# A soft mixture-of-experts behind linear attention: a fourth home for early weights, the last experts' products ahead of the first half's last chunks, 512-column zero products

## The chip, the core and the metric

The kernel runs on one core of a Trainium2 chip. The metric is the device time of one execution in microseconds, median of several runs. Before the change it is 177.03 us (three runs, 176.82 to 177.19).

## The reference

For 8 batches and 8 heads (sequence 576, head dimension 64) linear attention is computed, normalised, and handed as 4,608 tokens of 512 features to a soft mixture of 8 experts with 4 slots each. All data is 4-byte floating point.

```python
kv = np.einsum('bhsd,bhse->bhde', k, v)
out = np.einsum('bhsd,bhde->bhse', q, kv)
rms = np.sqrt(np.mean(out * out, axis=-1, keepdims=True) + 1e-06)
x = out / rms * g_norm                      # as 4608 tokens x 512
logits = x @ phi                            # 4608 x 32 slots
d = softmax(logits, over the tokens)
slot_input = d.T @ x                        # 8 experts x 4 slots x 512
h = np.maximum(slot_input[e] @ w1[e], 0.0)  # 512 x 1024 per expert
slot_out[e] = h @ w2[e]                     # 1024 x 512 per expert
c = softmax(logits, over the slots)
return c @ slot_out
```

## The kernel before, in words

The core reads 61.9 MB (k, v, q and the weights `w1`, `w2` of 4 MB per expert) and writes 9.4 MB. The work has two parts.

**The token part** goes over 36 tiles of 128 tokens (`products`, `square`, `evict` and what follows them). TensorE multiplies q by the block matrices `bds[0]` and `bds[1]`, ScalarE and VectorE find the norms, GpSimd scales, and the tokens of a group of six tiles are summed into slots (`group_sum`, L361) against a running maximum. The last group is the serial piece: its maximum is found (L317), transposed on TensorE (`pm`, L327), broadcast (`pb`, L342), subtracted and put through the exponential, and only then come the group's 48 small products (L361), their transpose (`psT`, L504) and the first expert. `fill` (L398) puts products of zeros on TensorE where it would otherwise stand idle: `EARLY` at the start, `LATE_FILL` in that serial piece. The first entry of `LATE_FILL` is 28 products of 256 columns, started when the sums of the group before are done; the next instruction of TensorE behind them is `pm`.

**The expert part** computes `expert_h(e)` (L567, from `w1`) and `expert_y(e, hf)` (L585, from `w2`, `hf` one half of the 512 output features). For the first four experts both halves of y follow at once; for the last four, half 0 comes first. Then `mix(0)` copies the sums out of PSUM (VectorE), spreads them with one product (`pz`, L602) and copies them back (`z`, L604). `output(hf, k, f)` makes one chunk of the result: two products pairs (`po`, L613), one copied by ScalarE (L621), one by VectorE (L623), into a tile `st`, and one transfer of 768 KB (L624). There are 12 chunks, six for each half. The table `late` places the last four `expert_y(e, 1)` between the first half's chunks; `mix(1)` follows all six.

**Transfers.** All of them are issued by SyncE in one order that is written out in the code: k, v and q, then the weights of experts 0 to 3, `w1` of 4 to 7, half 0 of `w2` of 4 to 7, half 1, and then the results as they come. SyncE works in order and waits for the semaphore of the transfer issued eight before, so at most eight are under way. Buffers: `ring` has 17 slots of 1 MB through which k, v, q, the weights and then the result tiles go; a new tile waits until the tile 17 before has been used. `w1` is loaded in two blocks of 1 MB per expert, k = 0 and 1. Three blocks don't use the ring: block (4, 0) lies in four 256 KB pieces in the small pool `rest` (`SPLIT`), and (5, 0) and (5, 1) in eight pieces in the token tiles `xts` that are done with (`IN_X`). `load_w1` (L72) issues all of them; a piece has rows of 2 KB, a whole block rows of 8 KB.

Of the kernel before, what the change touches and what calls it, by code (L numbers as in the profile page):

```python
# [8 lines left out]
F32 = mybir.dt.float32  # L9
# [5 lines left out]
P = 128  # L15
# [3 lines left out]
NE = 8  # L19
# [7 lines left out]
NCH = NT // CT  # L27
NX = 14
EARLY = (18, 2, 0)
LATE_FILL = (28, 5, 5, 2, 2)  # L30
PACED = 3
SLOT = 2048
NSLOT = 17
SPLIT = (4, 0)
IN_X = ((5, 0), (5, 1))
NREST = 5
EPS_RMS = 1e-6
EPS_SUM = 1e-9
# [3 lines left out]
def soft_moe_linear_attention(ctx: ExitStack, tc: tile.TileContext, kv_in, kvr_in, q_in, qr_in, w1_in, w2_in, c_in, out):  # L42


    nc = tc.nc

    const = ctx.enter_context(tc.tile_pool(name="const", bufs=1))
    ring = ctx.enter_context(tc.tile_pool(name="ring", bufs=NSLOT))
    rest = ctx.enter_context(tc.tile_pool(name="rest", bufs=NREST))
    wk = ctx.enter_context(tc.tile_pool(name="wk", bufs=2))  # L50
# [20 lines left out]

    def load_w1(e):  # L72
        for k in range(2):
            if (e, k) == SPLIT or (e, k) in IN_X:

                if (e, k) == SPLIT:
                    parts = [rest.tile([P, 512], F32, tag="rest", name=f"w1_{e}_{k}_{i}") for i in range(4)]
                else:
                    T = NT - GROUPS[-1] - 8 + 4 * IN_X.index((e, k))
                    parts = [xts[(T + i) % NX].rearrange("p j n -> p (j n)")[:, :512] for i in range(4)]  # L80
                for i, t in enumerate(parts):
                    nc.sync.dma_start(t, w1_in[e, k, :, i // 2, i % 2 * 512 : i % 2 * 512 + 512])
                w1_sb[e, k] = [[parts[2 * c + j // 2][:, j % 2 * 256 : j % 2 * 256 + 256] for j in range(4)] for c in range(2)]
                continue
            t = ring.tile([P, 2, FF], F32, tag="ring", name=f"w1_{e}_{k}")
            nc.sync.dma_start(t, w1_in[e, k])
            w1_sb[e, k] = [[t[:, c, j * 256 : (j + 1) * 256] for j in range(4)] for c in range(2)]
# [19 lines left out]
    zeros = const.tile([P, 256], BF16, name="zeros")  # L107
# [13 lines left out]
    bds = [const.tile([P, NPAIR, 192], F32, name=f"bd{i}") for i in range(2)]  # L121
# [3 lines left out]
    for i in range(NX):  # L125
        t = const.tile([P, 4, 129], F32, name=f"x{i}")
# [12 lines left out]
    ps = psA.enter_context(tc.tile_pool(name="psA", bufs=1, space=bass.MemoryType.PSUM))  # L139
# [69 lines left out]
    sqs, mss, parts, r0s, rs_of = {}, {}, {}, {}, {}  # L209
# [74 lines left out]
    def scale_o(T, o, of_x):  # L284

        s = stage_of[T]
        r = rs_of[s][:, T - starts[s]].rearrange("p (j w) -> p j w", w=2).unsqueeze(3)
        if of_x:
            out = xts[T % NX][:, :, :128].rearrange("p j (w d) -> p j w d", w=2)
            src = o[:, :, 32:160].rearrange("p j (w d) -> p j w d", w=2)  # L290
        else:
            parts[s] = wk.tile([P, STAGES[s], H, NS], F32, tag="part", name=f"part{s}", bufs=3)
            out = parts[s][:, T - starts[s]].rearrange("p (j w) n -> p j w n", w=2)
            src = o[:, :, :192].rearrange("p j (c n) -> p j c n", n=NS)[:, :, 0::5]
        nc.vector.tensor_tensor(out=out, in0=src, in1=r.to_broadcast([P, 4, 2, D if of_x else NS]), op=ALU.mult)
# [28 lines left out]
    def group_max_T(G):  # L324
        pm = ps.tile([P, P], F32, tag="m", name=f"pm{G}")
        for j in range(4):
            nc.tensor.matmul(  # L327
                pm[32 * j : 32 * j + 32], lhsT=L[:, pos(g0[G]) + GROUPS[G]], rhs=ident, start=True, stop=True
            )
        pms[G] = pm  # L330
# [9 lines left out]
    def group_exp_PE(G):  # L340
        pbs[G] = ps.tile([P, NS], F32, tag="m", name=f"pb{G}")
        nc.tensor.matmul(pbs[G], lhsT=ones, rhs=held[G], start=True, stop=True)  # L342
# [12 lines left out]
    def group_sum(G, i):  # L355
        if i == 0:
            sums[G] = ps.tile([P, 129], F32, tag="s", name=f"pS{G}")
        pS = sums[G]
        x = xts[(g0[G] + i) % NX]
        for j in range(4):  # L360
            nc.tensor.matmul(  # L361
                pS[32 * j : 32 * j + 32], lhsT=ds[G][:, i], rhs=x[:, j], start=i == 0, stop=i == GROUPS[G] - 1
            )
        if i == GROUPS[G] - 1:
            if G == 0:
                nc.vector.tensor_copy(out=acc, in_=pS)
            else:
                nc.vector.scalar_tensor_tensor(
                    out=acc, in0=acc, scalar=alphas.pop(G), in1=pS, op0=ALU.mult, op1=ALU.add
                )  # L370
# [27 lines left out]
    def fill(n, cols=256, home=None):  # L398

        if not n:  # L400
            return
        t = home if home is not None else ps.tile([P, 2, 512], F32, tag="o", name="fill", bufs=2)[:, 1]
        for i in range(n):
            nc.tensor.matmul(t[:, :cols], lhsT=zeros[:, :P], rhs=zeros[:, :cols], start=True, stop=True)

    fill(EARLY[0])

# [8 lines left out]
    for T in range(NT - 2):  # L416
# [15 lines left out]
        old = ends.get(T - 2)  # L432
# [50 lines left out]
    group_max(G)  # L483
    for i in todo_sums:
        group_sum(*i)
    fill(LATE_FILL[0], home=ps.tile([P, 256], F32, tag="m", name="fill"))
    group_max_T(G)
    group_max_row(G)
    group_diag(G)
    scale_o(A, oA, True)  # L490
    fill(LATE_FILL[1], home=tail_ps[:, 1])
    group_exp_PE(G)
    group_exp(G)
    scale_o(Z, oZ, True)
    fill(LATE_FILL[2], home=tail_ps[:, 1])
    for i in range(GROUPS[G]):
        group_sum(G, i)
    fill(LATE_FILL[3], home=tail_ps[:, 1])

# [4 lines left out]
    nc.tensor.transpose(psT, acc[:, :128], ident)  # L504
    fill(LATE_FILL[4], home=tail_ps[:, 1])
    mine = psT.rearrange("p (j e k) -> p e j k", j=4, k=SPE)
# [17 lines left out]
    ps = ctx.enter_context(tc.tile_pool(name="psB", bufs=3, space=bass.MemoryType.PSUM, reuse_waits="tile"))  # L524
    LATE = 4
# [55 lines left out]
    def expert_y(e, hf):  # L581
        w2 = w2_sb[e, hf]
        for c in range(8):
            j = c % 4
            nc.tensor.matmul(  # L585
                pY[32 * j : 32 * j + 32, hf, :256],
                lhsT=hTs[e][:, c],
                rhs=w2[:, c],
                start=e == 0 and c < 4,
                stop=e == NE - 1 and c >= 4,  # L590
            )
# [5 lines left out]
    def mix(hf):  # L597

        y = wk.tile([P, 256], F32, tag="part", name=f"y{hf}", bufs=3)
        nc.vector.tensor_copy(out=y, in_=pY[:, hf, :256])  # L600
        pz = ps.tile([P, 2, 512], F32, tag="m", name=f"pz{hf}")[:, 0, :256]
        nc.tensor.matmul(pz, lhsT=sel.rearrange("p a n -> p (a n)"), rhs=y, start=True, stop=True)  # L602
        zs[hf] = wk.tile([P, 256], F32, tag="part", name=f"z{hf}", bufs=3)
        nc.vector.tensor_copy(out=zs[hf], in_=pz)  # L604

    def output(hf, k, f):
        z = zs[hf]
        st = ring.tile([P, 4, CT * NS], F32, tag="ring", name=f"st{hf}_{k}_{f}")
        for v in range(2):
            po = ps.tile([P, 2, 512], F32, tag="m", name=f"po{hf}_{k}_{f}_{v}")  # L610
            for u in range(2):
                lo = 32 * (2 * v + u)
                nc.tensor.matmul(  # L613
                    po[:, u, : CT * NS].rearrange("p (g x) -> p g x", g=2),
                    lhsT=z[lo : lo + 32, f * P : (f + 1) * P],
                    rhs=cT[k][lo : lo + 32],
                    start=True,
                    stop=True,
                )
            if v == 0:  # L620
                nc.scalar.copy(st[:, 0:2], po[:, :, : CT * NS])  # L621
            else:
                nc.vector.tensor_copy(out=st[:, 2:4], in_=po[:, :, : CT * NS])  # L623
        nc.sync.dma_start(out[hf, k, f], st)  # L624
# [20 lines left out]
            keep_busy(PACED)  # L645
    mix(0)
    chunks = [(k, f) for k in range(NCH) for f in range(2)]
    late = {1: 0, 2: 1, 4: 2, 5: 3}
    for i, (k, f) in enumerate(chunks):
        output(0, k, f)  # L650
        if i in late:
            expert_y(NE - LATE + late[i], 1)
    mix(1)
    for k, f in chunks:
        output(1, k, f)

# [1 line left out]
def build_program():  # L658
    import concourse.bacc as bacc

    nc = bacc.Bacc("TRN2", target_bir_lowering=False, num_devices=1)
    shapes = {"kv": (B, 2, P, SLOT), "kr": (B, P, 512), "qt": (B, P, NPAIR, 512), "qr": (B // 2, P, 2, NPAIR, 64), "w1": (NE, 2, P, 2, FF), "w2": (NE, 2, P, 8, 256), "cs": (P, 129)}
    args = [nc.dram_tensor(f"in_{n}_dram", s, F32, kind="ExternalInput").ap() for n, s in shapes.items()]
    args.append(nc.dram_tensor("out_0_dram", (2, NCH, 2, P, 4, CT * NS), F32, kind="ExternalOutput").ap())
    with tile.TileContext(nc, schedule_with_timeline_sim=True) as tc, tc.manual_schedule():
        soft_moe_linear_attention(tc, *args)
    return nc
# [40 lines left out]
```

## Time and profile before

| | |
|---|---|
| median of the runs | 177.03 us (176.82 to 177.19) |
| profiled execution: time, span | 176.62 us, 174.8 us |
| busy, share of the span | PE 86%, VectorE 51%, ScalarE 50%, GpSimd 32% |
| transfers | 71.69 MB, mean 410 GB/s; SyncE's queue 98.6% of 16 engines |
| TensorE clock, mean | 0.976 of full speed |

The profiled execution took 176.62 us; 1.8 us of it lie outside the span from its first to its last instruction. A share of busy time is an average over the parts above. The row of the transfers in 40 slices shows 9 (90% or more) in every slice but the first and the last, at 375 to 433 GB/s.

### The profile page before, as it was taken

What the parts mean: (1) busy time and instruction counts of PE and PEld (TensorE: products, weight loads), DVE (VectorE), ACT (ScalarE), POOL (GpSimd) and SP (SyncE); (2) the same over time, 40 slices, a digit from 0 to 9 for tenths busy, and PEclk for the clock granted to TensorE, in tenths of its full rate; (3) what the DMA queues carried; (4) which work ended last, traced back from release to release, by engine and by line L of the source; (5) the groups of instructions that cost most, each with busy time, mean ns of one, the idle gap of its engine ahead of it and who ended that gap; (6) DMA issues with size and microseconds to landing.
All of it is one profiled execution on the core that took longest, in us unless ns stands there. A gap on an engine that the chain in (4) does not pass through costs nothing.

```text
span 174.8 us, 4903 instructions
## 1 busy us (share of the span) xinstructions
PE 150.5 (86%) x2040; PEld 110.5 (63%) x2040; DVE 88.7 (51%) x180; ACT 87.0 (50%) x224; POOL 56.0 (32%) x78
## 2 busy tenths in 40 slices
PE   7776999999989899999998868789979997987900
PEld 5465969898779788888986756556636542434300
DVE  1122165666466664657655679624886204553720
ACT  2116486879858958869777751102222303343600
POOL 7000246666556566464666565000000000000000
PEclk9999999999999999999999999789999999999995
DMA  5999999999999999999999999999999999999995
GB/s 191 424 424 415 426 433 420 416 422 427 427 420 418 422 419 427 420 426 424 429 420 427 424 427 419 417 397 382 422 422 424 418 431 422 425 424 375 422 425 250
DMA packets 12982, 71.69 MB, mean 410 GB/s; under 512 B 1440, under 2 KB 1568, under 8 KB 6176
## 3 DMA queue, kind: packets, MB, share of 16 engines
q1 hardware_dynamic: 12960, 71.37, 98.6%
q8 instruction: 16, 0.26, 0.5%
q14 instruction: 6, 0.05, 0.1%
HBM read 61.93 MB, written 9.44 MB: 408 GB/s over the span
## 4 chain that ended last, share of the span: by engine, by line
PE 52%; DVE 16%; ACT 12%; DMA 8%; issue 4%; POOL 2%; SPq 1%; POOLq 0%; DVEq 0%
PE o L227 17%; PE kvp_kv L159 8%; DMA kv<-in_kv_dram 8%; PE po L613 6%; PE ph L567 6%; PE pY L585 5%; DVE logits L304 3%; PE pS L361 2%; DVE ms L250 2%; POOL part L299 2%; ACT bd L194 2%; PE o L218 2%; ACT sq L237 2%; DVE st L623 2%; PE kvp_kv L174 2%
## 5 line engine op out<-in xcount | busy, mean ns | idle before, releaser
L227 PE MATMUL o<-bd,q 128*128 128x192 f32 x256 | 49.4, 336 | 1.5 <-ACT x L245 0.6
L227 PEld LDWEIGHTS o<-bd,q 128*128 128x128 f32 x256 | 40.8, 190 | 4.7 <-ACT x L245 1.6
L277 POOL TENSOR_TENSOR x<-x,r 128x512 f32<-128x512 f32 x34 | 34.7, 1043 | 0.0
L299 POOL TENSOR_TENSOR part<-part,r 128x512 f32<-128x512 f32 x17 | 17.8, 1048 | 50.3 <-DVE r L268 50.3
L304 DVE TENSOR_REDUCE logits<-part 128x64 f32<-128x512 f32 (+1 forms) x19 | 19.3, 1015 | 16.1 <-POOL part L299 16.0
L250 DVE TENSOR_REDUCE ms<-sq 128x16 f32<-128x1024 f32 (+1 forms) x19 | 22.0, 1157 | 6.3 <-ACT sq L237 6.3
L237 ACT ACTIVATE sq<-o 128x512 f32<-128x512 f32 x36 | 21.4, 596 | 6.6 <-PE o L227 6.0
L245 ACT COPY x<-o 128x512 f32<-128x512 f32 x34 | 20.6, 607 | 0.0
L159 PE MATMUL kvp_kv<-kv 128*64 128x64 f32 x480 | 17.4, 226 | 2.1 <-DMA kv<-in_kv_dram 2.1
L159 PEld LDWEIGHTS kvp_kv<-kv 128*64 128x64 f32 x480 | 15.4, 139 | 5.2 <-DMA kv<-in_kv_dram 3.0
L621 ACT COPY st<-po 128x768 f32<-128x768 f32 x12 | 9.3, 801 | 17.6 <-PE po L613 17.6
L585 PE MATMUL pY<-w,x 128*32 128x256 f32 x256 | 16.2, 382 | 1.2 <-DVE x L579 1.2
L623 DVE COPY st<-po 128x768 f32<-128x768 f32 x12 | 11.3, 956 | 8.4 <-PE po L613 8.4
L613 PE MATMUL po<-logits,z 32*128 32x384 f32 x96 | 13.5, 525 | 2.3 <-DVE z L604 1.1
L361 PE MATMUL pS<-x,d 128*32 128x129 f32 x288 | 12.0, 301 | 1.9 <-ACT d L349 1.9
L567 PE MATMUL ph<-w,sTe 128*32 128x256 f32 x224 | 13.0, 379 | 0.3 <-DVE sTe L508 0.3
L585 PEld LDWEIGHTS pY<-w,x 128*32 128x32 f32 x256 | 7.5, 109 | 8.6 <-issue 2.6
L244 ACT COPY part<-o 128x256 f32<-128x256 f32 x34 | 12.6, 371 | 0.0
L258 ACT ACTIVATE r<-ms,eps 128x16 f32<-128x16 f32 x17 | 5.2, 308 | 12.7 <-DVE ms L250 12.5
L613 PEld LDWEIGHTS po<-logits,z 32*128 32x128 f32 x96 | 5.7, 183 | 9.1 <-ACT st L621 3.8
L361 PEld LDWEIGHTS pS<-x,d 128*32 128x32 f32 x288 | 8.5, 119 | 4.5 <-issue 4.0
L575 ACT ACTIVATE h<-ph,rs 128x256 f32<-128x256 f32 x8 | 3.8, 472 | 14.1 <-PE ph L567 14.1
(90 smaller groups left out, 145.5 us busy)
## 6 DMA issues: line engine op xcount, KB each, us to landing
w<-in_w_dram SPq DMA_DIRECT2D x29, 1024.0 KB, 18.0
kv<-in_kv_dram SPq DMA_DIRECT2D x16, 1024.0 KB, 14.3
out_dram<-st SPq DMA_DIRECT2D x12, 768.0 KB, 5.5
q<-in_qt_dram SPq DMA_DIRECT2D x8, 1024.0 KB, 14.2
kvr<-in_kr_dram SPq DMA_DIRECT2D x8, 256.0 KB, 14.8
x<-in_w_dram SPq DMA_DIRECT2D x8, 256.0 KB, 7.3
qr<-in_qr_dram SPq DMA_DIRECT2D x4, 256.0 KB, 14.1
w<-in_w_dram SPq DMA_DIRECT2D x4, 256.0 KB, 15.0
```

The costliest lines, as they stand in the source:

```text
L159: nc.tensor.matmul(self.pkv[lo : lo + 64, w, g], lhsT=main[:, w, 1, c, lo : lo + 64], rhs=main[:, w, 0, c, lo : lo + 64], start=c == 0 and ...
L227: nc.tensor.matmul(o[:, r, :192], lhsT=q_sb[2 * g + i][:, r, at : at + P], rhs=bds[i][:, r], start=True, stop=True)
L237: nc.scalar.activation(sqs[s][:, T - starts[s]], o[:, :, 32:160], AF.Square, scale=0.125)
L245: nc.scalar.copy(xts[T % NX][:, :, :128], o[:, :, 32:160])
L250: nc.vector.tensor_reduce(out=mss[s], in_=sqs.pop(s).rearrange("p t j (w d) -> p (t j w) d", w=2), axis=AX.X, op=ALU.add)
L277: nc.gpsimd.tensor_tensor(out=x, in0=x, in1=r[:, i].rearrange("p (j w) -> p j w", w=2).unsqueeze(3).to_broadcast([P, 4, 2, D]), op=ALU.mult,)
L299: engine.tensor_tensor(out=part, in0=part, in1=rs_of[s].unsqueeze(3).to_broadcast([P, STAGES[s], H, NS]), op=ALU.mult)
L304: nc.vector.tensor_reduce(out=L[:, pos(starts[s]) : pos(starts[s]) + STAGES[s]], in_=parts.pop(s).rearrange("p t h n -> p t n h"), axis=AX ...
L361: nc.tensor.matmul(pS[32 * j : 32 * j + 32], lhsT=ds[G][:, i], rhs=x[:, j], start=i == 0, stop=i == GROUPS[G] - 1)
L567: nc.tensor.matmul(ph[32 * j : 32 * j + 32], lhsT=sTe[:, (4 * e + c) * NS : (4 * e + c + 1) * NS], rhs=w1[c % 2][j], start=c == 0, stop=c ...
L585: nc.tensor.matmul(pY[32 * j : 32 * j + 32, hf, :256], lhsT=hTs[e][:, c], rhs=w2[:, c], start=e == 0 and c < 4, stop=e == NE - 1 and c >= 4,)
L613: nc.tensor.matmul(po[:, u, : CT * NS].rearrange("p (g x) -> p g x", g=2), lhsT=z[lo : lo + 32, f * P : (f + 1) * P], rhs=cT[k][lo : lo + 32],
```

## The change

Four edits, and the constants that go with them. `load_w1` gives block (6, 0) a home outside the ring as well: two of its 256 KB pieces in `bds[0]` and `bds[1]`, two in one buffer of the pool tag `sq`. All later ring tiles move up by one slot. The first late fill becomes 21 products of 512 columns (the zeros repeated) in place of 28 of 256. `late` places the last experts' half-1 products after chunks 1, 1, 2 and 3, and `mix(1)` behind chunk 3.

```diff
-LATE_FILL = (28, 5, 5, 2, 2)
+LATE_FILL = (21, 5, 5, 2, 2)
+IN_BD = (6, 0)
...
-            if (e, k) == SPLIT or (e, k) in IN_X:
+            if (e, k) == SPLIT or (e, k) in IN_X or (e, k) == IN_BD:
...
+                elif (e, k) == IN_BD:
+                    old = wk.tile([P, 2, 512], F32, tag="sq", name="w1_sq")
+                    parts = [bds[i].rearrange("p j n -> p (j n)")[:, :512] for i in range(2)] + [old[:, i] for i in range(2)]
...
-            nc.tensor.matmul(t[:, :cols], lhsT=zeros[:, :P], rhs=zeros[:, :cols], start=True, stop=True)
+            nc.tensor.matmul(
+                t[:, :cols].rearrange("p (a n) -> p a n", n=256),
+                lhsT=zeros[:, :P],
+                rhs=zeros.unsqueeze(1).to_broadcast([P, cols // 256, 256]),
+                start=True,
+                stop=True,
+            )
...
-    fill(LATE_FILL[0], home=ps.tile([P, 256], F32, tag="m", name="fill"))
+    fill(LATE_FILL[0], home=ps.tile([P, 512], F32, tag="m", name="fill"), cols=512)
...
-    late = {1: 0, 2: 1, 4: 2, 5: 3}
+    late = {1: (0, 1), 2: (2,), 3: (3,)}
     for i, (k, f) in enumerate(chunks):
         output(0, k, f)
-        if i in late:
-            expert_y(NE - LATE + late[i], 1)
-    mix(1)
+        for j in late.get(i, ()):
+            expert_y(NE - LATE + j, 1)
+        if i == 3:
+            mix(1)
```

SyncE's order around block (6, 0), before (`w_6_0` from L86 is block (6, 0) of `w1`, `x_...` are pieces in token tiles):

```order
L82 DMA x_167<-in_w_dram 128x512
L82 DMA x_169<-in_w_dram 128x512
L86 DMA w_6_0_1596<-in_w_dram 128x2048
L86 DMA w_6_1_1598<-in_w_dram 128x2048
L86 DMA w_7_0_1600<-in_w_dram 128x2048
L86 DMA w_7_1_1602<-in_w_dram 128x2048
```

and with the change (lines move by four):

```order
L86 DMA x_167<-in_w_dram 128x512
L86 DMA x_169<-in_w_dram 128x512
L86 DMA bd_163<-in_w_dram 128x512
L86 DMA bd_164<-in_w_dram 128x512
L86 DMA w_sq<-in_w_dram 128x512 x2
L90 DMA w_6_1_1594<-in_w_dram 128x2048
L90 DMA w_7_0_1596<-in_w_dram 128x2048
```

One transfer of 1 MB has become four of 256 KB, at the same place in the queue, straight behind the eight pieces in token tiles; the transfers behind it keep their order.

TensorE's order behind the second chunk of half 0, before (`po_k_f_v` are the products of a chunk, `w_4_1` to `w_7_1` here half 1 of `w2` of experts 4 to 7):

```order
L585 MATMUL pY<-w_4_1_1612,x_177 32x256 x8
L613 MATMUL po_1_0_0_1957<-logits,z_1926 128x384 x2
L613 MATMUL po_1_0_1_1961<-logits,z_1926 128x384 x2
L585 MATMUL pY<-w_5_1_1614,x_177 32x256 x8
L613 MATMUL po_1_1_0_1975<-logits,z_1926 128x384 x2
L613 MATMUL po_1_1_1_1979<-logits,z_1926 128x384 x2
L613 MATMUL po_2_0_0_1985<-logits,z_1926 128x384 x2
L613 MATMUL po_2_0_1_1989<-logits,z_1926 128x384 x2
L585 MATMUL pY<-w_6_1_1616,x_175 32x256 x8
L613 MATMUL po_2_1_0_2003<-logits,z_1926 128x384 x2
L613 MATMUL po_2_1_1_2007<-logits,z_1926 128x384 x2
L585 MATMUL pY<-w_7_1_1618,x_175 32x256 x8
```

and with the change:

```order
L595 MATMUL pY<-w_4_1_1608,x_177 32x256 x8
L595 MATMUL pY<-w_5_1_1610,x_177 32x256 x8
L623 MATMUL po_1_0_0_1961<-logits,z_1922 128x384 x2
L623 MATMUL po_1_0_1_1965<-logits,z_1922 128x384 x2
L595 MATMUL pY<-w_6_1_1612,x_175 32x256 x8
L623 MATMUL po_1_1_0_1979<-logits,z_1922 128x384 x2
L623 MATMUL po_1_1_1_1983<-logits,z_1922 128x384 x2
L595 MATMUL pY<-w_7_1_1614,x_175 32x256 x8
L612 MATMUL pz_1998<-y_1996,sel 128x256
L623 MATMUL po_2_0_0_2003<-logits,z_1922 128x384 x2
L623 MATMUL po_2_0_1_2007<-logits,z_1922 128x384 x2
```

The product of `mix(1)` (`pz`) now stands ahead of the fifth and sixth chunk of half 0, not behind them. On VectorE the two copies of `mix(1)` move in the same way ahead of those chunks' copies.

## Rows read from the trace of the kernel before

**Rows 1.** Waits of SyncE's queue: who waited for what, us in total, times, longest.

```profile
SPq L665 <- DMA out_dram<-st: 5.7, 1, 5.7
```

**Rows 2.** Windows: stretch, its us, busy us (instructions) per engine, clock, DMA share, GB/s.

```profile
20.00:40.00 20.00, 19.64 (x258) 16.95 (x256) 11.72 (x22) 15.22 (x43) 12.20 (x12) 1.00 1.02 424
...
118.00:119.00 1.00, 1.00 (x24) 0.63 (x20) 0.00 (x0) 0.29 (x1) 0.00 (x0) 1.00 1.06 363
119.00:120.00 1.00, 1.00 (x28) 0.59 (x20) 0.45 (x1) 0.19 (x1) 0.00 (x0) 1.00 1.05 340
...
160.00:161.00 1.00, 0.76 (x8) 0.30 (x6) 0.87 (x1) 1.00 (x2) 0.00 (x0) 1.00 0.89 369
161.00:162.00 1.00, 1.00 (x12) 0.52 (x8) 0.34 (x1) 0.47 (x2) 0.00 (x0) 1.00 0.69 289
```

**Rows 3.** SyncE's timeline, seven short windows: start us, us, engine, line, operation, names.

```profile
107.35 0.33 SPq L82 DMA_DIRECT2D x<-in_w_dram  x1
...
109.38 0.33 SPq L82 DMA_DIRECT2D x<-in_w_dram  x1
...
116.85 0.33 SPq L82 DMA_DIRECT2D x<-in_w_dram  x1
...
132.14 0.33 SPq L91 DMA_DIRECT2D w<-in_w_dram  x1
...
157.16 0.33 SPq L624 DMA_DIRECT2D out_dram<-st  x1
...
160.93 0.33 SPq L624 DMA_DIRECT2D out_dram<-st  x1
...
167.33 0.74 SPq L624 DMA_DIRECT2D out_dram<-st  x1
```

**Rows 4.** Transfers issued in the same seven windows, in order: KB, us to landing.

```profile
x<-in_w_dram SPq DMA_DIRECT2D x1, 256.0 KB, 10.1
...
x<-in_w_dram SPq DMA_DIRECT2D x1, 256.0 KB, 9.0
...
x<-in_w_dram SPq DMA_DIRECT2D x1, 256.0 KB, 5.5
...
w<-in_w_dram SPq DMA_DIRECT2D x1, 1024.0 KB, 19.5
...
out_dram<-st SPq DMA_DIRECT2D x1, 768.0 KB, 5.6
...
out_dram<-st SPq DMA_DIRECT2D x1, 768.0 KB, 3.6
...
out_dram<-st SPq DMA_DIRECT2D x1, 768.0 KB, 6.5
```

**Rows 5.** TensorE's rows of the timeline in the serial piece, idle time and its end in brackets.

```profile
103.89 1.53 PE L361 MATMUL pS<-x,d 128*32 128x129 f32 x48 [1.71 <-ACT d L349]
...
105.35 3.23 PE L404 MATMUL fill<-zeros 128*128 128x256 bf16 x28
...
109.98 0.43 PE L327 MATMUL pm<-ident,logits 128*32 128x128 f32 x8 [1.40 <-DVE logits L317]
...
112.50 2.79 PE L361 MATMUL pS<-x,d 128*32 128x129 f32 x48 [0.16 <-ACT d L349]
```

**Rows 6.** Windows ahead of and in that piece, columns as in rows 2.

```profile
109.00:110.00 1.00, 0.02 (x3) 0.05 (x5) 0.96 (x3) 0.00 (x0) 0.00 (x0) 1.00 1.00 404
...
112.00:113.00 1.00, 0.84 (x14) 0.53 (x16) 0.56 (x1) 0.54 (x2) 0.00 (x0) 0.50 1.10 451
```

**Rows 7.** The chain that ended last, at the results: start us, us, what.

```profile
148.66 1.00 PE pY L585 x16
149.66 0.86 PE po L613 x8
...
157.11 0.44 DVE y L600
157.59 0.71 PE pz L602 x2
158.32 0.44 DVE z L604
158.90 0.93 PE po L613 x8
```

## The prediction

> **What bounds the kernel now.** I read the waits of SyncE first: after its last issue it does nothing for 5.7 us but wait for results to land [rows 1]. So the end is set by transfers, not by the engines that made the last chunk. Then the windows: a quiet stretch moves 424 GB/s at a full DMA share, and only two short stretches fall visibly below it, 118 to 120 us (363 and 340 GB/s) and 160 to 162 us (369 and 289) [rows 2]. If those dips are lost time, the change can win them back; if not, it has nothing to win.
>
> The issues and their landings answer this. The last piece of block (5, 1) is issued at 116.85 and lands 5.5 us later, at 122.35; the last result is issued at 167.33 and lands 6.5 us later, at 173.83 [rows 3, 4]. In these 51.5 us land 12 blocks of 1 MB and 12 results of 768 KB, 22.02 MB, that is 428 GB/s, though the dip of 160 to 162 lies between. That is no less than the quiet rate, so nothing was lost. The dip itself shows how: the result issued at 157.16 lands at 162.76, the next, issued only at 160.93, at 164.53 [rows 3, 4]. The step is 1.77 us, and 786 KB at 424 GB/s need 1.85. Transfers landed without a gap while the share fell to 0.69. My reading: the 16 DMA engines are not level; those that are ahead run dry in a dip, those that are behind never stop, and a transfer counts as landed with its last engine. The engines behind set the end of the kernel. The Trainium skill ("DMA: Bandwidth & Descriptors", the section on why a DMA increments its semaphore by 16) says that the engines of a transfer finish independently and that only the full count means landed; the landings of this trace agree with it, 1.77 us apart through a dip in the share.
>
> So the chain of waits, which runs mostly over TensorE, misleads here: it passes through work that is done 6.5 us before the end.
>
> **The change, part by part.**
>
> *Block (6, 0) in four pieces.* The bytes are the same, the number of transfers grows by three. Lower bound of a piece: 262 KB at the quiet 424 GB/s, 0.62 us, which makes four of them as dear as the block (2.47 us), a cost of nothing. Upper bound: the eight pieces in token tiles land from 117.45 (issued 107.35, 10.1 us) to 122.35, seven steps in 4.9 us, 0.70 each [rows 3, 4]; four cost 2.80, 0.33 more than the block. One step of these seven is an odd one: the second piece, issued 109.38, lands at 118.38, 0.93 behind the first. The other six take 3.97, 0.66 each. The new pieces stand right behind them and have the same rows of 2 KB, so I take 0.66: 4 x 0.66 - 2.47 = **+0.17 us**, and every landing behind them is later by it. A saving below zero is excluded, since no piece can land faster than the quiet rate.
>
> *The earlier slots.* SyncE's later loads no longer wait for the experts' products to free a slot. But they are issued with transfers still queued ahead of them, and nothing lands earlier for it: 0.
>
> *21 products of 512 columns.* The 28 old ones take 3.23 us, 115 ns each, and end at 108.58; `pm` starts at 109.98 [rows 5]. TensorE is busy for 0.02 us between 109 and 110, and by 112 to 113 its granted clock is 0.50, that is 1.2 GHz [rows 6]. The 48 sums there take 2.79 us, against 1.53 for the same 48 at full clock [rows 5]: 1.26 us. No 512-column product is in the trace. At most one costs twice the old one, 231 ns; at least 512 columns at 2.4 GHz, 213. So the fill ends between 109.83 and 110.2, up to 0.2 us behind the present start of `pm`, and the idle stretch ahead of the fall is gone. I take it that the clock stays up: TensorE's work behind it comes **1.1 us earlier**. For the end that is worth 0, as the transfers cover it: weights are landing until 151.64 (issued 132.14, 19.5 us later [rows 3, 4]) whatever TensorE does.
>
> *Order of the results.* Behind the second chunk TensorE stands at 148.66; a `pY` group takes 1.00 and a chunk of half 0 there 0.86 [rows 7]. The new order gives two groups (150.66), chunk (151.52), group (152.52), chunk (153.38), group (154.38), and then `mix(1)`. Before, the copy of `mix(1)` starts at 157.11 and the first result behind it is issued at 160.93, 3.82 us later [rows 3, 7]. Now that result is the fifth chunk of half 0. It needs only TensorE, not the second `z`, so it saves up to 0.6 us (from the start of that copy at 158.32 to the products at 158.90 [rows 7]). It is issued at 157.6 to 158.2, and 1.1 earlier with the clock held: **156.5 to 157.1**. When must it be? Before, a result issued 1.83 us ahead of its predecessor's landing (160.93 against 162.76) left no gap. The fourth result lands two steps of 1.85 ahead of 162.76, at 159.06, and 0.17 later with the pieces; the fifth must be issued by 157.4. It just makes it, with 0.3 to 0.9 to spare. The last `pY` group, at 152.3, finds its weights landed at 151.8. The dip of 160 to 162 goes away: 0 us, as above.
>
> **Sum:** 176.62 (profiled) + 0.17 + 0 + 0 = 176.8 us, with a span of 175.0. The median of the runs is 0.41 above the profiled execution, so it becomes **177.2 us**.
>
> By the Trainium skill's rule ("DMA: Bandwidth & Descriptors", § Bandwidth) to batch transfers to 1 MiB or more, with that page's fit of 2.0 us fixed per transfer plus bytes over 436 GB/s, four pieces in sequence would cost 10.4 us against 4.4, +6 us, an estimate. The trace speaks against it for queued pieces: 0.70 us each at most.
>
> **Rivals.**
>
> *The dips did cost (faster).* If the engines were level after all, the 160 to 162 dip is worth (55 + 135)/424 = 0.45 us, and the 118 to 120 dip (61 + 84)/424 = 0.34, of which perhaps half goes, as slow pieces fill the place. 177.03 + 0.17 - 0.45 - 0.17 = 176.6 us. For it: both dips are real and the change acts on both. Against it: 428 GB/s of landings across the second one.
>
> *The fifth result comes late (slower).* `mix(1)` now stands ahead of it on TensorE and VectorE. If the clock falls in spite of the fill, it is issued at 157.6 to 158.2 against a need of 157.4: 0.2 to 0.8 us in which every DMA engine stands still, taken as 0.5. 177.03 + 0.17 + 0.5 = 177.7 us. It decides at an issue later than 157.4.
>
> *The pieces starve the queue (slower).* Twelve pieces now follow one another, and SyncE issues each only when the one eight before has landed, so 2 MB are under way where 8 were. If the 118 to 120 loss (0.34 us in 2) spreads over the 2.6 us of the new ones, that is 0.45 more: 177.03 + 0.17 + 0.45 = 177.65 us. Against it: seven queued pieces are 4.6 us of work, and the 160.93 issue shows that 1.83 are enough.
>
> *The fill does not hold the clock, without more:* the times of the forecast, since that gain is hidden.
>
> **How the numbers follow.** Forecast 0.62, dips paid 0.18, fifth result late 0.10, starved queue 0.10. A measurement of this kernel tells changes above 0.2%, 0.35 us, from none, so 176.68 and 177.38 are the limits. The forecast of 177.2, with bounds of 177.03 to 177.36 for the pieces, lies between them except for a tail; the dips paid land below for the greater part, the other two above. Faster 0.16, same 0.62, slower 0.22. The range takes in the forecast with its bounds, half of the first rival and nearly all of the others: 176.65 to 177.7.
>
> **What would show it.** Right: pieces that land 0.66 us apart, four more of them; clock 1.00 from 112 to 115 and the 48 sums in about 1.5 us; no dip at 160 to 162; the fifth result issued near 156.8; SyncE's last wait longer than 5.7 us, by about what the results are earlier; the end no earlier. Wrong: a span under 174.5, with landings of the results less than 1.8 us apart or an earlier last weight; or a landing gap of over 2 us ahead of the fifth result, or of over 0.8 us among the pieces.

## The result, and the profile after

| | before | with the change |
|---|---|---|
| median | 176.93 us (6 runs, 176.59 to 177.32) | 177.62 us (6 runs, 177.48 to 178.23) |
| ratio, 95% interval | | 1.0043 [1.0023, 1.0063] |
| profiled execution: time, span | 176.62, 174.8 us | 177.63, 175.9 us |

The change makes the kernel slower, by 0.69 us between the medians and 0.43% by the ratio (in the text below, differences in us are those of the medians): inside the range, but not the likeliest case, which was the same time. The time is that of the third rival, the queue starved by pieces.

The page of the profile shows what the case is about in one row: the transfers, in 40 slices of 4.4 us.

```profile
GB/s 179 431 419 413 437 424 418 419 425 425 419 423 427 416 418 426 423 425 423 429 423 425 423 427 421 417 391 347 388 416 429 423 427 421 424 417 420 423 425 201
```

The 27th to 29th slice (114 to 127 us) fall to 391, 347 and 388 GB/s. The windows of the stretch, with columns as in [rows 2]:

```profile
20.00:60.00 40.00, 38.66 (x501) 33.07 (x500) 24.15 (x47) 31.55 (x88) 24.39 (x24) 1.00 1.02 423
...
118.00:119.00 1.00, 1.00 (x28) 0.58 (x20) 0.45 (x1) 0.20 (x1) 0.00 (x0) 1.00 0.98 371
119.00:120.00 1.00, 1.00 (x24) 0.59 (x20) 0.09 (x1) 0.47 (x1) 0.00 (x0) 1.00 1.01 373
120.00:121.00 1.00, 1.00 (x24) 0.64 (x20) 0.97 (x3) 0.00 (x0) 0.00 (x0) 1.00 1.01 371
121.00:122.00 1.00, 1.00 (x28) 0.57 (x22) 0.45 (x1) 0.52 (x1) 0.00 (x0) 1.00 0.99 361
122.00:123.00 1.00, 1.00 (x24) 0.61 (x20) 0.87 (x3) 0.12 (x2) 0.00 (x0) 1.00 0.91 293
123.00:124.00 1.00, 1.00 (x25) 0.62 (x20) 0.93 (x3) 0.39 (x1) 0.00 (x0) 1.00 0.83 299
124.00:125.00 1.00, 1.00 (x28) 0.57 (x23) 1.00 (x3) 0.00 (x0) 0.00 (x0) 1.00 0.94 373
...
160.00:162.00 2.00, 1.97 (x14) 0.93 (x14) 1.20 (x2) 1.56 (x3) 0.00 (x0) 1.00 1.02 424
```

Up to 122 the rate is low at a DMA share of about 1.00: the engines work, at 361 to 373 GB/s, on rows of 2 KB. From 122 to 125 the share itself falls, to 0.83: engines stand still. Against the quiet 424 [rows 2] those three windows miss 131 + 125 + 51 GB/s times 1 us, or 0.72 us of transfer time. The packets of the trace say the same without windows. Counted every 10 ns, there are nearly always 16 packets of 512 B or more under way, as many as there are engines; what is missing to 16, as a share of 16, adds up to 0.05 us over the 40 us from 20 to 60, but to 0.64 us over 116 to 128, with only 10 under way at the lowest. Before, the same 12 us miss 0.09 us. The three microseconds from 122 to 125 in the kernel before:

```profile
122.00:125.00 3.00, 3.00 (x64) 1.80 (x56) 2.24 (x6) 1.03 (x2) 0.00 (x0) 1.00 1.02 418
```

The dip of 160 to 162 [rows 2] is gone, as forecast: 424.

Whether a dip costs time is told by the landings. SyncE's timeline with the change (start, us, engine, line), single issues, then the same issues with KB and us to landing:

```profile
117.67 0.33 SPq L86 DMA_DIRECT2D bd<-in_w_dram  x1
...
118.40 0.33 SPq L86 DMA_DIRECT2D bd<-in_w_dram  x1
...
119.06 0.33 SPq L86 DMA_DIRECT2D w_sq<-in_w_dram  x1
...
119.67 0.33 SPq L86 DMA_DIRECT2D w_sq<-in_w_dram  x1
...
120.39 0.33 SPq L90 DMA_DIRECT2D w<-in_w_dram  x1
...
121.71 1.35 SPq L90 DMA_DIRECT2D w<-in_w_dram  x1
...
154.10 0.33 SPq L634 DMA_DIRECT2D out_dram<-st  x1
...
157.20 0.33 SPq L634 DMA_DIRECT2D out_dram<-st  x1
...
166.53 0.35 SPq L634 DMA_DIRECT2D out_dram<-st  x1
```

```profile
bd<-in_w_dram SPq DMA_DIRECT2D x1, 256.0 KB, 5.3
...
w_sq<-in_w_dram SPq DMA_DIRECT2D x1, 256.0 KB, 5.2
...
w_sq<-in_w_dram SPq DMA_DIRECT2D x1, 256.0 KB, 5.5
...
w<-in_w_dram SPq DMA_DIRECT2D x1, 1024.0 KB, 7.6
...
w<-in_w_dram SPq DMA_DIRECT2D x1, 1024.0 KB, 11.2
...
out_dram<-st SPq DMA_DIRECT2D x1, 768.0 KB, 5.9
...
out_dram<-st SPq DMA_DIRECT2D x1, 768.0 KB, 4.8
...
out_dram<-st SPq DMA_DIRECT2D x1, 768.0 KB, 8.3
```

Issue plus time to landing: the four pieces (the second `bd` takes 5.3 as well) land at 123.0, 123.7, 124.3 and 125.2, and block (6, 1) at 128.0. So the last piece is 0.9 behind the third, where the others are 0.6 to 0.8 apart, and a block of 1 MB then takes 2.8 us where the quiet rate gives 2.47. Block (7, 1), two later, lands at 132.9; before, the same block was issued at 120.39 and landed 11.7 later, at 132.1:

```profile
120.39 0.33 SPq L86 DMA_DIRECT2D w<-in_w_dram  x1
```

```profile
w<-in_w_dram SPq DMA_DIRECT2D x1, 1024.0 KB, 11.7
```

That 0.8 us, of which 0.2 was there ahead of the first old piece already (it lands 10.2 us after its issue at 107.44, at 117.6, not 117.45), stays to the end. The fourth result lands at 160.0 (154.10 + 5.9) and the last at 174.8 (166.53 + 8.3): eight steps in 14.8 us, 1.85 each on average, the quiet pace. The first of the eight is longer: the fifth result lands at 162.0 (157.20 + 4.8), 2.1 behind the fourth in the trace. That is, by a hair, the sign that the prediction named for a late fifth result; the steps behind it are 1.80 to 1.84 and make it good. The last landing was 173.83 before [rows 3, 4], so the end is 1.0 later, although SyncE issues the last result 0.8 us earlier (166.53 against 167.33). Its last wait grows from 5.7 [rows 1] to 6.1:

```profile
SPq L676 <- DMA out_dram<-st: 7.9, 2, 6.1
```

The landings also show how uneven the engines are. The trace holds 16 increments of the semaphore for each transfer, and the last of them is the landing. For the first old piece the first increment comes 2.9 us ahead of the last, in both kernels. So of the 5.3 us that the new pieces take to land, the engines that are ahead use less than 3: the first increments of the four come 2.4 to 2.9 us after the issue, and the shortest such time of any transfer in these runs is 2.0. Before, only the last old piece comes near that (2.55); there the lead shrinks, for the first increment of the next block comes 3.15 us behind that of the piece, while the last increments keep the quiet 2.44.

TensorE did what was forecast. Its timeline in the serial piece, to be held against [rows 5]:

```profile
105.49 4.71 PE L408 MATMUL fill<-zeros 128*128 128x512 bf16 x21
...
110.25 0.43 PE L331 MATMUL pm<-ident,logits 128*32 128x128 f32 x8
...
112.79 1.53 PE L365 MATMUL pS<-x,d 128*32 128x129 f32 x48 [0.39 <-ACT d L353]
```

A 512-column product takes 4.71/21 = 224 ns, `pm` starts 0.27 us later, and the 48 sums take 1.53 us in place of 2.79. For the end of the kernel that gave nothing.

### The profile page after: what moved, and what is told of

Read it like the earlier page. It is cut to its first block, busy times and chain, and to the rows that moved or that the text cites. A ratio compares the mean times of both kernels' runs of the same rounds, so it can differ in the third digit from the quotient of the medians.

```text
span 175.9 us, 4893 instructions
## 1 busy us (share of the span) xinstructions
PE 150.2 (85%) x2033; PEld 108.5 (62%) x2033; DVE 88.7 (50%) x180; ACT 87.0 (49%) x224; POOL 56.0 (32%) x78
## 4 chain that ended last, share of the span: by engine, by line
PE 48%; DMA 18%; DVE 12%; ACT 10%; issue 3%; POOL 2%; SPq 1%; POOLq 0%; DVEq 0%
PE o L231 17%; DMA w<-in_w_dram 10%; PE kvp_kv L163 8%; DMA kv<-in_kv_dram 8%; PE po L623 6%; PE pY L595 4%; PE ph L577 3%; DVE logits L308 3%; DVE st L633 2%; PE pS L365 2%; DVE ms L254 2%; POOL part L303 2%; ACT bd L198 2%; PE o L222 2%; ACT sq L241 2%
## 5 line engine op out<-in xcount | busy, mean ns | idle before, releaser
L365 PE MATMUL pS<-x,d 128*32 128x129 f32 x288 | 10.7, 276 | 2.1 <-ACT d L353 2.1
L577 PE MATMUL ph<-w,sTe 128*32 128x256 f32 x208 | 12.2, 379 | 0.3 <-DVE sTe L518 0.3
L270 DVE SCALAR_TENSOR_TENSOR r<-ms,r 128x16 f32<-128x16 f32 x17 | 3.0, 175 | 14.9 <-ACT r L263 14.9
L365 PEld LDWEIGHTS pS<-x,d 128*32 128x32 f32 x288 | 7.4, 109 | 4.5 <-issue 4.1
## 6 DMA issues: line engine op xcount, KB each, us to landing
kvr<-in_kr_dram SPq DMA_DIRECT2D x8, 256.0 KB, 14.8
```

The costliest lines, as they stand in the source:

```text
L365: nc.tensor.matmul(pS[32 * j : 32 * j + 32], lhsT=ds[G][:, i], rhs=x[:, j], start=i == 0, stop=i == GROUPS[G] - 1)
L577: nc.tensor.matmul(ph[32 * j : 32 * j + 32], lhsT=sTe[:, (4 * e + c) * NS : (4 * e + c + 1) * NS], rhs=w1[c % 2][j], start=c == 0, stop=c ...
```

## The experiments

Two explanations stood against each other. **Q**: SyncE keeps at most eight transfers under way; twelve small ones in a row leave only 2 MB queued, the DMA engines run dry, and that time is lost to every landing behind. **M**: `mix(1)` ahead of the fifth result makes that result late. Two more were kept beside them: that the rows of 2 KB cost by themselves, and that the new buffers (`bds`, `sq`) do. All ratios are to the kernel before, run on the same chip with them.

| run | edit | median, before | ratio [95%] |
|---|---|---|---|
| e1 | pieces only | 178.05, 176.99 | 1.0054 [1.0035, 1.0074] |
| e2 | order only | 177.03, 176.99 | 1.0003 [0.9989, 1.0017] |
| e3 | wide fill only | 176.90, 176.99 | 0.9996 [0.9983, 1.0009] |
| e4 | all but the pieces | 177.16, 176.99 | 1.0006 [0.9992, 1.0020] |
| e5 | pieces spread out | 177.92, 177.02 | 1.0046 [1.0029, 1.0063] |
| e6 | pieces in a ring slot | 177.59, 177.02 | 1.0041 [1.0021, 1.0061] |
| e7 | quarters of 32 partitions | 181.65, 177.02 | 1.0253 [1.0216, 1.0289] |
| e8 | pieces merged by two | 177.74, 177.02 | 1.0029 [1.0012, 1.0046] |
| e9 | expert 5's pieces joined, block (6, 0) whole | 179.60, 177.13 | 1.0143 [1.0116, 1.0170] |
| e10 | expert 5's joined, the four pieces kept | 179.43, 177.13 | 1.0143 [1.0118, 1.0168] |
| e11 | all joined | 179.77, 177.13 | 1.0159 [1.0135, 1.0182] |
| e12 | as e10, every buffer at its old place | 176.89, 176.96 | 0.9992 [0.9976, 1.0008] |

### The parts of the change (e1 to e4)

e1 keeps the home of block (6, 0) and undoes the order and the fill:

```diff
-LATE_FILL = (21, 5, 5, 2, 2)
+LATE_FILL = (28, 5, 5, 2, 2)
...
-    late = {1: (0, 1), 2: (2,), 3: (3,)}
+    late = {1: (0,), 2: (1,), 4: (2,), 5: (3,)}
...
-        if i == 3:
+        if i == 5:
```

> Only block (6, 0) in four pieces outside the ring; order of the results and late fill as before. If the pieces starve the queue (theory Q), most of the loss is here: +0.5 to +0.8 us against the kernel before, and the DMA rate falls below 320 GB/s for about 2 us between 121 and 125 us. If the pieces cost only their 2 KB rows (theory R), +0.15 to +0.2 us and no such dip. If the fifth result's lateness makes the loss (theory M), no more than +0.2 us here.

It has the whole loss and more, +1.06 us, above the 0.5 to 0.8 that Q expected, though the interval overlaps that of the whole change. Its windows and the issues of its two last pieces:

```profile
122.00:123.00 1.00, 1.00 (x25) 0.57 (x21) 0.38 (x2) 0.55 (x1) 0.00 (x0) 1.00 1.01 346
123.00:124.00 1.00, 1.00 (x24) 0.65 (x20) 0.90 (x4) 0.47 (x1) 0.00 (x0) 1.00 0.72 221
124.00:125.00 1.00, 1.00 (x28) 0.58 (x20) 0.97 (x3) 0.00 (x0) 0.00 (x0) 1.00 0.87 291
```

```profile
119.66 0.33 SPq L86 DMA_DIRECT2D w_sq<-in_w_dram  x1
...
120.28 0.33 SPq L86 DMA_DIRECT2D w_sq<-in_w_dram  x1
```

```profile
w_sq<-in_w_dram SPq DMA_DIRECT2D x1, 256.0 KB, 5.2
...
w_sq<-in_w_dram SPq DMA_DIRECT2D x1, 256.0 KB, 6.1
```

They land at 124.9 and 126.4, a gap of 1.5 us for 256 KB, and the share falls to 0.72 just there; by the packets 0.81 us of 16 engines are missing over 116 to 128. The order is the old one, so M has no part in it.

e2 takes the change without the pieces and with the old fill (`IN_BD = None`, 28 products of 256 columns); e3 has the wide fill alone (`IN_BD = None`, the old `late`); e4 is the change with one line undone:

```diff
-IN_BD = (6, 0)
+IN_BD = None
```

> Only the new places of the last experts' products and of mix(1); block (6, 0) in the ring and the late fill of 28 x 256 columns as before. Theory Q: no loss, 0.0 us (-0.1 to +0.1); theory M: a landing step of over 2.0 us ahead of the fifth result and +0.2 us or more, since without the fill TensorE is about 1 us later than in the whole change, so the fifth result is issued near 158.2. The dip at 160 to 162 us should be gone and be worth nothing.

> Only the late fill of 21 x 512 columns. All theories: clock 1.00 from 112 to 115 us, the first expert about 1 us earlier, and no change of the time (-0.1 to +0.1 us), since transfers cover it. If TensorE's end counted, it would be up to 1 us faster.

> The whole change without the pieces: block (6, 0) in its ring slot, new order and new fill. Theory Q: about the time before, -0.1 to +0.2 us; theory M: +0.2 us, with the late fifth result in the landings; if the parts only hurt together, near the kernel before as well and e1 and e2 too.

None of the three differs from before, by intervals of about 0.14% to either side. As the cause of the loss M is out: the 0.2 us that it expected is no more than such an interval, but in the traces of e2 and e4 the fifth result lands 1.86 and 1.88 us behind the fourth, the quiet pace. The fill is worth nothing. e4 against the change is the cleanest cut: one line, and the loss is gone. What e2 shows beside that belongs to the clock:

```profile
105.48 3.23 PE L408 MATMUL fill<-zeros 128*128 128x256 bf16 x28
...
110.11 0.43 PE L331 MATMUL pm<-ident,logits 128*32 128x128 f32 x8 [1.40 <-DVE logits L321]
112.64 1.53 PE L365 MATMUL pS<-x,d 128*32 128x129 f32 x48 [0.39 <-ACT d L353]
```

```profile
112.00:115.00 3.00, 2.41 (x56) 1.65 (x53) 1.05 (x3) 0.55 (x2) 0.00 (x0) 1.00 1.03 424
```

With the old fill and the same idle 1.40 us ahead of `pm` as in [rows 5], the 48 sums take 1.53 us and the granted clock of 112 to 115 is 1.00; the profile of e1, which has the old fill too, shows the same. So the fall to 0.50 [rows 6] is in one profile of three with that fill, and that the wide fill is what holds the clock is not shown.

### Spreading, another home, other shapes (e5 to e8)

e5 issues the four pieces one at a time, each behind one of the next blocks of 1 MB (`one_piece()` stands behind the loads of `w2` as well):

```diff
+                    if (e, k) == IN_BD:
+                        held_back.append((t, w1_in[e, k, :, i // 2, i % 2 * 512 : i % 2 * 512 + 512]))
+                        continue
...
             nc.sync.dma_start(t, w1_in[e, k])
+            one_piece()
```

> The whole change, but the four pieces of block (6, 0) are issued one by one between the 1 MB blocks behind them, not in a row behind the eight pieces in token tiles. Theory Q (too few bytes under way while twelve pieces follow one another): most of the loss goes, to 0.1 to 0.3 us above the kernel before. Theory B (the buffers they are written to, or their 2 KB rows as such, cost the time): the loss stays at 0.6 us or more.

By Q the loss should have gone. It stayed, +0.90 us, but at another place, 119 to 122 where expert 5's eight pieces land:

```profile
119.00:120.00 1.00, 1.00 (x26) 0.57 (x22) 0.08 (x1) 0.19 (x1) 0.00 (x0) 1.00 1.02 307
120.00:121.00 1.00, 1.00 (x24) 0.64 (x20) 0.69 (x2) 0.28 (x1) 0.00 (x0) 1.00 1.08 277
121.00:122.00 1.00, 1.00 (x28) 0.59 (x20) 0.82 (x2) 0.11 (x1) 0.00 (x0) 1.00 0.85 336
```

A miss for Q as it stood: the row of twelve is broken up here, and the loss is the same. Most of it falls at a full share (307 and 277 GB/s at 1.02 and 1.08), and only the last of the three windows has a low one (0.85). The packets tell more. Over 116 to 128 they miss 0.30 us of 16 engines, a third of the loss; much of the rest shows as packets of 8 KB that take up to 1.9 us between 119 and 121, where a quiet one takes 0.31. Both lie where the engines ahead pass from the last old piece to the next block: the first increment of that piece comes at 119.7, 2.1 us after its issue, so these engines had run out before the first of the new pieces could matter. Why e5 loses so much more there than e4, which has the same old pieces, is not settled.

e6 puts the four pieces, with the same rows of 2 KB, into an ordinary ring slot:

```diff
-            nc.sync.dma_start(t, w1_in[e, k])
+            if (e, k) == (6, 0):
+                for i in range(4):
+                    at = i % 2 * 512
+                    nc.sync.dma_start(t[:, i // 2, at : at + 512], w1_in[e, k, :, i // 2, at : at + 512])
```

> New order and fill, block (6, 0) back in its ring slot, but carried by four transfers of 256 KB with 2 KB rows at the same place in the queue. Theory Q: the loss is back, +0.5 to +0.9 us against the kernel before, with landing steps of over 0.8 us among or just behind the pieces. Theory B as to buffers: no loss, within 0.2 us.

+0.57 us, as the change, with the same dip: 290 GB/s over 122 to 125 at a share of 0.85, and by the packets 0.73 us of 16 engines missing over 116 to 128.

```profile
122.00:125.00 3.00, 3.00 (x64) 1.81 (x60) 2.86 (x7) 0.47 (x1) 0.00 (x0) 1.00 0.85 290
```

So it is neither the buffers nor the ring slots that move up, but the four small transfers.

e7 was to part the number of transfers from the length of their rows: four transfers of 32 partitions with rows of 8 KB.

```diff
+                for i in range(4):
+                    nc.sync.dma_start(t[32 * i : 32 * i + 32], w1_in[e, k, 32 * i : 32 * i + 32])
```

> As e6_ring_pieces, but the four transfers are cut by partitions: 32 partitions each with whole rows of 8 KB. Theory Q: number and size of the transfers count, so +0.4 to +0.7 us, less than e6 by the 0.1 to 0.2 us that 2 KB rows cost. If the short rows make the loss: within 0.2 us of the kernel before.

It could not: +4.6 us, far outside what either theory expected.

```profile
122.00:125.00 3.00, 3.00 (x64) 1.81 (x60) 2.60 (x7) 0.70 (x2) 0.00 (x0) 1.00 1.03 219
```

219 GB/s at a full share of 1.03 is half the quiet rate with no engine idle: another limit, brought in by the shape. The Trainium skill ("SBUF — State Buffer", Door 1: The DMA port swizzle) says that a transfer's bandwidth depends on how many of 16 ports its partitions reach, and by its table 32 neighbouring partitions reach eight; the half rate agrees with it. One block of 1 MB at that rate would cost 2.4 us; the low rate lasts from 121 to 128, and why it reaches beyond the four transfers is not shown. As a test of Q the run is void.

e8 moves block (6, 0) in two transfers of 512 KB (`bds` as one tile, the `sq` half in one piece):

```diff
+                if (e, k) == IN_BD:
+                    both = bd_all.rearrange("p i j n -> p i (j n)")[:, :, :512]
+                    nc.sync.dma_start(both, w1_in[e, k, :, 0].rearrange("p (i n) -> p i n", i=2))
+                    nc.sync.dma_start(old.rearrange("p i n -> p (i n)"), w1_in[e, k, :, 1])
```

> The whole change, but block (6, 0) in two transfers of 512 KB (the two block matrices as one tile, rows of 2 KB; the pool buffer with rows of 4 KB). Theory Q: half the number, double the bytes under way, so most of the loss goes: 0.1 to 0.4 us above the kernel before. Theory B: the loss stays at 0.6 us or more.

1.0029, between before and the change, and +0.72 us by the medians, above the 0.1 to 0.4 that Q expected. Its interval overlaps those of both e4 and e6, so by itself it decides nothing.

### Joining the pieces ahead of them (e9 to e12)

If Q holds, the four pieces must become free when those ahead of them are large. e9 to e11 lay the token tiles in one tile and load expert 5's two blocks with three transfers (1 MB, 512 KB, 512 KB) in place of eight; e9 without the pieces of (6, 0), e10 with them, e11 with them merged as in e8.

```diff
+    x_all = const.tile([P, NX, 4, 129], F32, name="x")
...
-        t = const.tile([P, 4, 129], F32, name=f"x{i}")
+        t = x_all[:, i]
...
+                    rows = x_all.rearrange("p t j n -> p t (j n)")[:, :, :512]
...
+                        nc.sync.dma_start(rows[:, at : at + n], src[:, i : i + n])
```

> New order and fill, block (6, 0) in its ring slot, and the eight pieces of expert 5's blocks joined to three transfers (1 MB, 512 KB, 512 KB) with the same rows of 2 KB into the same buffers, which needs the token tiles in one tile. Theory Q (SyncE holds eight transfers, so small ones leave few bytes under way and DMA engines run dry): the dip at 118 to 121 us, which the kernel before has too, goes; the time is that of e4_no_pieces or up to 0.4 us less (176.6 to 177.1). Theory B (short rows into these buffers cost the time, whatever the transfers): dip and time stay as in e4_no_pieces (177.1).

> The whole change with its four pieces for block (6, 0), but expert 5's eight pieces joined to three transfers. Theory Q: only four small transfers in a row are left behind 2 MB of large ones, so the engines don't run dry: 0.1 to 0.3 us above e9_x_joined, for the short rows. Theory B: 0.6 us or more above it.

> The whole change with block (6, 0) in two transfers of 512 KB and expert 5's blocks in three. Theory Q: as e10 or 0.1 us less, 0.0 to 0.2 us above e9_x_joined, no stretch under 380 GB/s between 116 and 126 us. Theory B: 0.6 us or more above e9_x_joined.

All three came out some 2.5 us slower than was expected of e9. Against each other they already speak for Q: e10 with its four pieces takes 0.17 us less than e9 without them, and e11 0.17 us more, where theory B asked for 0.6 or more; two windows of e11, 117 to 119, are under the 380 GB/s that Q named, at 356 and 375. The windows show that the 2.5 us are not the pieces'; e9:

```profile
20.00:60.00 40.00, 38.68 (x495) 33.29 (x497) 24.12 (x47) 31.61 (x89) 24.42 (x24) 1.00 1.02 414
```

414 GB/s against 423 already from 20 to 60 us, long before any piece of `w1` is issued, at the same share of 1.02. What differs there is where things lie: a token tile has 2,064 bytes of data in a partition, the 14 single tiles were laid out 2,080 apart, and in the joined tile they are 2,064 apart, so that everything behind, the ring among it, begins 224 bytes lower (at byte 61,472 of a partition instead of 61,696, by the addresses in the built programs). e12 is e10 with 2,080 bytes per token tile, which puts every buffer back:

```diff
-    x_all = const.tile([P, NX, 4, 129], F32, name="x")
+    x_all = const.tile([P, NX, 520], F32, name="x")
...
-        t = x_all[:, i]
+        t = x_all[:, i, :516].rearrange("p (j n) -> p j n", n=129)
```

> As e10_x_joined_pieces (all of the change with its four pieces, expert 5's eight pieces joined to three transfers), but the token tiles keep the 2080 bytes apart that they had, so every buffer behind them lies where it lay before; in e9 to e11 the ring began 224 bytes lower, at an odd multiple of 32. If the places made the 2.5 us of e9 to e11: landings of 1 MB are back from 2.49 to 2.44 us apart, and by theory Q the time is within 0.25 us of the kernel before (176.8 to 177.3), 0.4 to 0.7 us under the whole change, with no landing step out of line among the pieces. If the joined transfers themselves are slow: 179 us or more again. Theory B: 177.6 us.

176.89 us against 176.96 before: the 2.5 us are gone, and the cost of the pieces with them. The interval, -0.24% to +0.08%, leaves out the change's +0.43%. Its windows, two issues, and the times to landing:

```profile
20.00:60.00 40.00, 38.65 (x498) 33.16 (x496) 24.13 (x47) 31.55 (x89) 24.40 (x24) 1.00 1.02 422
...
122.00:125.00 3.00, 3.00 (x64) 1.80 (x59) 2.58 (x7) 0.72 (x2) 0.00 (x0) 1.00 1.03 416
```

```profile
115.23 0.42 SPq L95 DMA_DIRECT2D w_sq<-in_w_dram  x1
...
117.22 0.33 SPq L99 DMA_DIRECT2D w<-in_w_dram  x1
```

```profile
x<-in_w_dram SPq DMA_DIRECT2D x1, 1024.0 KB, 12.3
x<-in_w_dram SPq DMA_DIRECT2D x2, 512.0 KB, 11.0
bd<-in_w_dram SPq DMA_DIRECT2D x2, 256.0 KB, 10.4
w_sq<-in_w_dram SPq DMA_DIRECT2D x2, 256.0 KB, 10.0
```

The four pieces are the same four transfers of 256 KB into the same buffers as in the change. They now wait 10.0 to 10.4 us for their landing, not 5.3: twice as much is queued ahead of them. 122 to 125 moves 416 GB/s at a share of 1.03, and block (6, 1), at 127.6 (117.22 + 10.4), lands 2.4 behind the last piece (115.23 + 10.0), the quiet pace. No engine is idle (0.01 us of 16 missing over 116 to 128), and the first increments of the pieces come 6.5 to 7.1 us after their issue, not 2.4 to 2.9. So the cost of the pieces lies in what is queued ahead of them and not in the pieces, as Q says. One rival is left, the number of small transfers, which e12 changes too: seven stand in the row where the change has twelve. No run here parts the two for good, and e5, with more bytes under way (3.5 MB issued and not landed at 120.5, against 2.75) and still twelve small transfers, loses as much.

## Why the prediction was wrong in its likeliest case, and right around it

**The step that failed** is the price of the pieces, and in it one sentence of the third rival: "seven queued pieces are 4.6 us of work, and the 160.93 issue shows that 1.83 are enough". The term was +0.17 us, with bounds of 0 and 0.33, worked out from the pace of the eight old pieces. It measured +1.06 alone (e1) and +0.69 in the whole change. Two faults lie in that sentence. The case at 160.93 was a short one, a single late issue with large transfers before and behind it, and it was carried over to a row of twelve small ones. And 4.6 us of queued work was read as a reserve, though it was a ceiling: with eight under way and 0.66 us each, a piece can have no more than 5.3 us ahead of it, which is just the 5.3 us that the pieces took to land. For the engines that are ahead by 2.9 us it is less than 3, and that is about the least that an issue takes to its first increment. The prediction itself had said that the engines are not level, and did not take the lead off the reserve. In that state the share fell to 0.83. Even the DMA engines that are behind then lost time: the signs named beforehand as "wrong", a gap of over 0.8 us among the pieces, came (0.9 here, 1.5 in e1), and 2.8 us for the block behind them. Why the engines behind lose, whose next transfers had been issued 4 us and more earlier, is not shown.

The old pieces already came near this state. My reading, which no run parts, is that the dip of 118 to 120 [rows 2] is the start of it, and that with eight pieces it ended before the engines behind were reached, with twelve not. The increments of before fit it (3.15 us for the engine ahead, 2.44 for the last); the full share of those two windows, 1.06 and 1.05, does not show it. The prediction ruled out a loss there with the 428 GB/s of landings, but these begin at 122.35, behind that dip: the count covers the dip of 160 to 162 alone. How much must be under way is not worked out here, and e5, which loses as much without the row of twelve, shows that the count of small transfers in a row is not the whole of it.

**The rival was sized from the right place.** It spread the loss of 118 to 120 over the new pieces and came to 177.65; the median is 177.62. That the two meet so closely is luck in part: the pieces alone cost 1.06 (e1), and the 0.45 was scaled from windows with a full share, where the loss of the change is mostly at a low one. The rival was given 0.10, because of the sentence above. The 0.17 us that the forecast put on the pieces' own pace is not seen in the time: e12, which has them, lies between -0.4 and +0.1 us of before. In the landings of e12 the four take 2.58 us, 0.65 each, as forecast. That this is the price of rows of 2 KB is another matter: in the ring slot of e6 the first three pieces, with the same rows, land 0.62 to 0.67 apart, and in before the four of block (4, 0) 0.60 to 0.64.

**The Trainium skill's rule** ("DMA: Bandwidth & Descriptors", § Bandwidth) to batch transfers to 1 MiB was set aside with the argument that queued pieces cost 0.70 us at most. The +6 us that the prediction estimated from that page's fit, which the page gives for transfers issued by GpSimd where here SyncE issues them, is not what is measured, +0.69; the direction of the rule is, and e12 gives the condition in this kernel: the same pieces cost nothing measurable behind large transfers.

**What held.** The transfers set the end: TensorE's last sums end at 114.3 instead of 115.3, 1.0 us earlier (1.1 forecast), the last result is issued 0.8 us earlier, and the end is 1.0 later. The fill: 224 ns per product (213 to 231 forecast) and `pm` 0.27 us later, a little more than the 0.2 allowed, the 48 sums in 1.53 us, worth 0 (e3). The order of results: the fifth is issued at 157.20, 0.1 behind the 156.5 to 157.1 forecast, worth 0 (e2, e4). The dip of 160 to 162 is filled and gives nothing back, which bears out the reading that such a short dip is not lost time, and the first rival, that the dips are paid, falls. The fall of the clock was read as a property of the old fill; by e1 and e2 it is not one of every execution, which changed no number, since it was costed at nothing.

No version that was run is faster than the kernel before beyond its interval.

## What to carry to other kernels

Where one queue holds a fixed number of transfers, count the time that the bytes under way will last, for the engine that is furthest ahead, and not the transfers: a row of small ones shrank the queue here to 5.3 us, less than 3 for the engines ahead, and a home for early data that has to be filled in pieces cost 0.7 us and gave none back. Read the landings, not the share alone: the dip at 160 cost nothing and the one at 122 cost 0.7 us, and the steps between landings told which (1.8 us for a result through the one, as in the quiet; 2.8 for a block behind the other, in place of 2.47). When a kernel is bound by transfers, costing an edit by its own pace is not enough; ask what is queued at the moment it runs.

## What was not expected of the hardware

- **Places in SBUF.** With token tiles 2,064 bytes apart and the ring 224 bytes lower, the whole kernel moves 414 GB/s instead of 423 and takes 2.5 us more (e10 against e12: 1.0143 against 0.9992). 61,696 is a multiple of 256 and 61,472 only of 32; that this is the cause was not tried apart, since e12 put back both the tiles' distance and the ring.
- **A quarter of the partitions.** Transfers of 32 partitions ran at 219 GB/s at a full share (e7).
- **The clock** fell to 0.50 in the profile of before and stayed at 1.00 in those of e1 and e2, with the same fill and the same idle 1.40 us ahead of `pm`.
